# Attention scores stored through a second DMA queue, and a weight product computed in another order from an earlier step

## The chip, the cores and the metric

The kernel runs on one core of one Trainium2 chip. The metric is the device time of one execution in microseconds (us); lower is better. Three runs of the kernel before took 1441.49, 1444.0 and 1446.57 us, median 1444.0.

## The reference

Attention with two mixings across heads, then a gated expert network whose last two weights have nothing between them (batch 8, 12 heads, 448 rows, head width 64; model width 768, inner width 1024):

```python
scores = scale * np.matmul(q, k.transpose(0, 1, 3, 2))
scores = np.einsum('bhij,hg->bgij', scores, w_pre)
scores = scores - np.max(scores, axis=-1, keepdims=True)
attn = np.exp(scores)
attn = attn / (np.sum(attn, axis=-1, keepdims=True) + 1e-09)
attn = np.einsum('bhij,hg->bgij', attn, w_post)
x = np.matmul(attn, v)                 # (8, 12, 448, 64) -> (3584, 768)
a = x @ w1
b = x @ w2
h = a * b @ w3
out = h @ w_out
```

The weights w1, w2, w3 and w_out are float64 on the host and reach the chip as pairs of 32-bit words. The kernel makes a float32 of each value, and of that a high and a low part in float32r.

## The kernel before

**The loop.** The attention goes in steps, 45 for each batch of ten score rows over all 12 heads, 360 in all; `run` writes the order of every engine's instructions out by hand. Batch 0's first score tiles are made ahead of the loop. A step issues, in this order: at even steps the fetch of two later row tiles from DRAM (`fetch`, line 202, tiles r); what was put off in the list `later` (score stores among it); loads of the rest of batch 0's kq, of v and of later kq; the first half of one weight conversion; the minimum over a row tile (even steps) or the scaling (odd); the second half of the conversion; some background matmuls; the exponentials (line 235, even steps); more background matmuls; the products with v (lines 301) at a few odd steps; at odd steps the post matmuls of the last pair (line 260) and the pre-mix of the next (line 220); and last the score units of this step.

**Score units.** A unit (`qk`) is two heads by 128 score rows: eight matmuls (line 174) into two PSUM banks, two copies on ScalarE into a tile st (lines 179 and 180), and a store to DRAM (`raw_d`, lines 185 and 188). A batch has 21 units, six sets of three and three smaller ones that store in two pieces. The tiles st come from rings of two. The store isn't issued where the copies are: `qk` returns it as a function, the loop puts it into `later`, and the next step issues it on SyncE's queue (SP) behind the fetch. All transfers of the kernel go out on SP. Batch 0's units go one to a step at steps 0 to 14; batch 1's begin at step 11, one every 4/3 steps; each batch's kq loads come six steps ahead of their first unit.

**The fold.** w3 and w_out are multiplied into one weight while the attention of batch 0 runs. `fold_jobs` lists 40 loads and conversions: the first eighth of w3's columns (three jobs), w_out in two halves of columns of eight jobs each, the other seven eighths of three jobs each. `converting` makes one a step (squaring and a cast on ScalarE, four passes on VectorE, the low part on GpSimd, line 130), save at steps with v products. `folding` then makes, for each eighth and each half of w_out's columns, 24 matmuls (line 360): eight blocks of the inner width, three products of parts each. 16 groups make 384 matmuls. The result goes through a tile fz to DRAM.

**The planner.** Three things decide how many fold matmuls a step gets. `shares(FOLD, SWITCH - 1, ...)` (line 847) deals all but 24 of them over steps 18 to 48 so that the steps come out level against the score units, v products and post and mix matmuls they also have. `there(p)` (line 865) caps what is done by the conversions made up to the step before; p counts the conversions. The first 24 may go ahead of the dealing. At step 50 (`SWITCH`) the fold must be done; the expert network's matmuls follow as background.

**Ahead of the loop**, rows 0 to 47 of batch 0's first score tiles are stored first, and the other 80 rows of all heads by one transfer (line 805, called at 881) behind the first two fetches.

Of the kernel before, what the change touches and what calls it, by code (L numbers as in the profile page):

```python
# [6 lines left out]
F32 = mybir.dt.float32  # L7
F32R = mybir.dt.float32r
I32 = mybir.dt.int32
AF = mybir.ActivationFunctionType  # L10
ALU = mybir.AluOpType
# [9 lines left out]
NB = -(-S // IB)  # L21
QT, NJ = 128, 4
GB = 15
NG = NB // GB
KF, K1 = FF // 128, DM // 128
IH = IB // 2
HK = H * IH
PP = 64
JB = S // PP
SETS = NB * B // 2  # L30
FIRST = 48
CW = 384
DH = DM // 2
LATE = 2 * NB + GB + 2
PAIRS = ((0, 0), (0, 1), (1, 0))
# [15 lines left out]
class Kernel:  # L51
# [114 lines left out]
    def qk(self, b, p, c, banks):  # L166


        nc = self.nc
        ps = [self.bank(i, f"psq{b}_{p}_{c}_{s}")[:, :S] for s, i in enumerate(banks)]  # L170
        for z, (t, q, k) in enumerate(self.parts(b, p, c)):
            for s in range(2):
                rows = slice(s * D, (s + 1) * D)
                nc.tensor.matmul(ps[s][z * PP:(z + 1) * PP], t[rows, q:q + PP], t[rows, k:k + S], start=True, stop=True)  # L174
        if b == c == 0:
            st = self.sz[:, 2 * p:2 * p + 2]
        else:
            st = (self.qp if b == 0 and p % 2 else self.kp).tile([128, 2, S], F32, tag="st", name=f"st{b}_{p}_{c}", bufs=2)
        nc.scalar.copy(st[:, 0], ps[0])  # L179
        (nc.vector.tensor_copy if b == c == 0 else nc.scalar.copy)(st[:, 1], ps[1])  # L180
        raw = self.raw_d[b]
        if c == 3:
            def store():
                for z in range(2):
                    nc.sync.dma_start(raw[3 * QT:, 2 * (p + z) - 2:2 * (p + z)], st[z * PP:(z + 1) * PP])
            return store
        n = QT if b or c else FIRST
        return lambda: nc.sync.dma_start(raw[c * QT:c * QT + n, 2 * p:2 * p + 2], st[:n])

# [137 lines left out]
    def fold_jobs(self):  # L329
        self.fo = self.fp.tile([128, KF, 2, DM], F32R, tag="o", name="fo", bufs=1)  # L330
        w3 = self.w_src[2].rearrange("(k p) f -> p k f", p=128)
        columns = [[(w3[:, k, f * 256:(f + 1) * 256], lambda x, f=f, k=k: self.fold_part(x, f, k))
                    for k in (slice(0, 3), slice(3, 6), slice(6, 8))] for f in range(KF)]
        yield from columns[0]
        for q in range(2):
            for k in range(KF):
                src = self.w_src[3][k * 128:(k + 1) * 128, 2 * q * DH:2 * (q + 1) * DH]
                hi, lo = (self.fo[:, k:k + 1, t, q * DH:(q + 1) * DH] for t in range(2))
                yield src.rearrange("p (a n) -> p a n", a=1), lambda x, hi=hi, lo=lo: self.two_parts(x, hi, lo)
        for f in range(1, KF):  # L340
            yield from columns[f]

    def fold_part(self, x, f, k):
# [2 lines left out]
        self.two_parts(x, *(self.fw[f][:, k, t] for t in range(2)))  # L346

    def folding(self):
        nc = self.nc
        for f in range(KF):  # L350
            for half in range(2):
                w = self.fw[f]

                i = 6 + half
                p = self.bank(i, f"psf{half}_{f}")[:, :DH]
                atoms = [(k, t, x, y) for k in range(KF) for t, (x, y) in enumerate(PAIRS)]
                for k, t, x, y in atoms:
                    if (k, t) != (0, 0):
                        yield
                    nc.tensor.matmul(p, w[:, k, x], self.fo[:, k, y, half * DH:(half + 1) * DH],  # L360
                                     start=(k == 0 and t == 0), stop=(k == KF - 1 and t == 2))
                z = self.fp.tile([128, 3, 2, 128], F32R, tag="z", name=f"fz{half}_{f}")
                q = p.rearrange("p (d c) -> p d c", c=128)
                dst = self.w34_d[half * 3:(half + 1) * 3, :, f].rearrange("d p t c -> p d (t c)")

                def low(z=z, q=q, dst=dst):
                    nc.vector.tensor_tensor(z[:, :, 1], q, z[:, :, 0].bitcast(F32), op=ALU.subtract)
                    self.later.append(lambda: nc.sync.dma_start(dst, z.rearrange("p d t c -> p d (t c)").bitcast(F32)))

                self.ends.append((i, lambda z=z, q=q: nc.scalar.copy(z[:, :, 0], q)))  # L370
                self.soon.append((i, low))
                yield

# [365 lines left out]
    def run(self):  # L741
        nc, tc = self.nc, self.tc
# [33 lines left out]
        w = self.kp.tile([128, 2, S], F32, tag="st", name="wpre_s", bufs=2)[:, 0, :PP]  # L776
# [18 lines left out]
        held = []  # L795
# [6 lines left out]
        next(fold_pieces)  # L802
        for f in held:
            f()
        held = lambda: nc.sync.dma_start(self.raw_d[0][FIRST:QT], self.sz[FIRST:])

# [1 line left out]
        for n, u in enumerate([(0, p, c) for c in (1, 2) for p in range(HP)] + [(0, p, 3) for p in range(1, HP, 2)]):  # L810
            qks[n] = [u]
        for b in range(1, B):
            first, per = (11, 28 / 21) if b == 1 else ((b - 1) * NB - 6, NB / 21)
            units = [(b, p, c) for g in range(0, HP, 2) for p, c in [*itertools.product((g, g + 1), range(3)), (g + 1, 3)]]
            for i, (b, p, c) in enumerate(units):
                n = int(first + i * per) | (b > 1)
                qks.setdefault(n, []).append((b, p, c))
                if c == 0:
                    loads.setdefault(max(n - 6, 0), []).append((b, p))
        for b in range(B):  # L820
            for a in range(NG):
                for g in range(HP):
                    n = (b * NB + (a + 1) * GB + 3) | 1
                    avs.setdefault(n if g < 3 else n + 2, []).append((b, a, g))

        N = B * NB
        FOLD, SWITCH, E_AT = 18, NB + 5, NB + 8
        PAIR, P_AT = 4 * NB + 7, 4 * NB + 15
        P_1 = 7 * 3 * (2 * K1 // 2 * KF // 2 + KF // 2 * K1 // 2)
        E_1, E_2 = 2 * KF * K1 * 3, K1 * KF * 3  # L830
# [18 lines left out]
        for pair in range(ONE // 2, B // 2 - 1):  # L849
            first = P_AT if pair == ONE // 2 else 2 * NB * (pair + 1) + 13  # L850
# [3 lines left out]
        background, total, done = self.folding(), F_N, 0  # L854
# [9 lines left out]

        def there(p):

            f, r = divmod(p - 3 - 2 * KF, 3)
            return 2 * KF * 3 * (1 + f) + (0, 9, 18)[r] if f >= 0 else min(max(3 * (p - 3), 0), KF * 3)

        wanted, LF = 0, 4  # L870
        self.v_list = [(b, g) for b in range(B) for g in range(HP)]
# [6 lines left out]
            self.fetch(m)  # L878
        next(fold_pieces)
        next(fold_pieces)  # L880
        held()
        next(fold_pieces)
        next(fold_pieces)
        self.mix(0)
# [4 lines left out]
        for n in range(N + 6):  # L889
# [4 lines left out]
            if n == SWITCH:  # L894
# [10 lines left out]
                background, total, done = self.experts(phases), (E_1 + E_2) * ONE + P_1 * (B - ONE) // 2, 0  # L905
# [29 lines left out]
            p, pieces = self.n_made - 1 if fold_pieces else 2 * KF + 3 * KF, None  # L935
            if avs.get(n):
                pass
            elif fold_pieces:
                f = (self.n_made - 1 - 2 * KF) // 3
                if f < 2 or done >= 2 * KF * 3 * (f - 1):  # L940
                    pieces = fold_pieces
                    if next(pieces, self) is self:
                        fold_pieces = pieces = None
# [18 lines left out]
            if n < SWITCH:  # L962

                wanted += now
                now = max(min(there(p), KF * 3 + wanted) - done, 0)
# [13 lines left out]
                self.mix(m + 1)  # L979
            self.do_ends()  # L980
            for i, x in enumerate(qks.get(n, [])):
                self.later.append(self.qk(*x, (6, 7) if i else (0, 1)))
            if third:
                next(unit_pieces)

# [66 lines left out]
```

## Time and profile before

| what | value |
|---|---|
| median of three runs | 1444.0 us (1441.49 to 1446.57) |
| the profiled execution | 1437.83 us, span 1436.1 us |
| TensorE matmul busy | 1382.4 us (96%) |
| ScalarE, VectorE, GpSimd busy | 832.4, 741.1, 620.3 us |
| mean granted TensorE clock | 0.986 |
| transfers | 416.87 MB, mean 290 GB/s |

The numbers come from one execution, profiled on the chip. Where a row has a start and a duration, both are in us from the start of the span. PE is TensorE's matmul row, PEld its weight loads, DVE VectorE, ACT ScalarE, POOL GpSimd, SP SyncE; SPq is SP's queue, which mostly issues transfers. A busy share is an average over stages, and busy TensorE isn't TensorE at full clock: PEclk tells what clock the throttle granted. A view by stretches gives, for each stretch, busy time and instruction count of each engine, the clock, the busy share of the 16 transfer engines and GB/s. A row of waits reads "engine line <- releaser: us in total, times, longest".

### The profile page before, as it was taken

What the parts mean: (1) busy time and instruction counts of PE and PEld (TensorE: products, weight loads), DVE (VectorE), ACT (ScalarE), POOL (GpSimd) and SP (SyncE); (2) the same over time, 40 slices, a digit from 0 to 9 for tenths busy, and PEclk for the clock granted to TensorE, in tenths of its full rate; (3) what the DMA queues carried; (4) which work ended last, traced back from release to release, by engine and by line L of the source; (5) the groups of instructions that cost most, each with busy time, mean ns of one, the idle gap of its engine ahead of it and who ended that gap; (6) DMA issues with size and microseconds to landing.
All of it is one profiled execution on the core that took longest, in us unless ns stands there. A gap on an engine that the chain in (4) does not pass through costs nothing.

```text
span 1436.1 us, 45775 instructions
## 1 busy us (share of the span) xinstructions
PE 1382.4 (96%) x18684; PEld 1055.2 (73%) x18684; DVE 741.1 (52%) x1497; ACT 832.4 (58%) x1952; POOL 620.3 (43%) x754
## 2 busy tenths in 40 slices
PE   5889999999999999999999999999999999999998
PEld 2457786776677667776777777777777777899988
DVE  6867566767544544432444436334444446345563
ACT  4867666777766666665656556556555445422231
POOL 2433233434433544532345336334335446446693
PEclk7989999999999999999999999999999999999999
DMA  8998789999999999999989979799879757698775
GB/s 294 366 326 279 236 270 322 320 312 317 324 286 348 355 356 330 362 346 349 287 275 290 320 259 280 249 323 354 288 229 281 241 177 223 195 337 270 231 232 171
DMA packets 203761, 416.87 MB, mean 290 GB/s; under 512 B 20528, under 2 KB 120112, under 8 KB 203472
## 3 DMA queue, kind: packets, MB, share of 16 engines
q1 hardware_dynamic: 203552, 413.94, 87.6%
q8 instruction: 149, 2.44, 0.7%
q14 instruction: 60, 0.49, 0.1%
HBM read 279.77 MB, written 134.09 MB: 288 GB/s over the span
## 4 chain that ended last, share of the span: by engine, by line
PE 82%; DMA 8%; DVE 4%; ACT 2%; issue 1%; POOL 1%; SPq 0%; DVEq 0%; POOLq 0%; ACTq 0%
PE e L702 21%; PE psa L301 11%; PE pso L260 10%; PE psm L220 9%; PE psq L174 7%; PE eg L522 5%; PE psf L360 4%; PE eo L553 4%; PE e2o L702 4%; PE e1o L702 4%; PE e3o L702 4%; DMA wu<-w_d 3%; DMA r<-raw_d 2%; DMA raw_d<-st 2%; ACT e L235 1%
## 5 line engine op out<-in xcount | busy, mean ns | idle before, releaser
L247 POOL TENSOR_SCALAR w<-wpo,ri 128x60 f32<-128x60 f32 x360 | 180.7, 518 | 485.1 <-DVE ri L245 465.3
L227 DVE TENSOR_REDUCE mn<-psm 128x1 f32<-128x448 f32 x360 | 207.7, 618 | 321.6 <-PE psm L220 321.3
L274 ACT COPY mt<-pso 128x480 f32<-128x480 f32 x352 | 197.9, 621 | 185.8 <-PE pso L260 185.6
L702 PE MATMUL e<-eh,wu 128*128 128x448 f32 x1008 | 296.8, 371 | 6.4 <-DVE c L656 3.2
L235 ACT ACTIVATE e<-psm,mn 128x448 f32<-128x448 f32 x360 | 226.8, 643 | 7.9 <-DVE mn L227 7.9
L702 PEld LDWEIGHTS e<-eh,wu 128*128 128x128 f32 x1008 | 187.5, 188 | 52.2 <-issue 26.8
L260 PEld LDWEIGHTS pso<-w,e 60*64 60x64 f32 x10080 | 175.2, 135 | 51.0 <-issue 42.5
L220 PE MATMUL psm<-r,wsc 60*64 60x448 f32 (+1 forms) x1440 | 191.2, 550 | 19.1 <-DVE cx L124 8.3
L260 PE MATMUL pso<-w,e 60*64 60x60 f32 x10080 | 199.1, 224 | 0.4 <-ACT mt L274 0.3
L702 PE MATMUL e<-el,wu 128*128 128x448 f32 x504 | 186.9, 371 | 0.0
L301 PE MATMUL psa<-mt,v 128*64 128x150 f32 (+1 forms) x2304 | 156.9, 292 | 4.1 <-ACT st L179 4.1
L301 PEld LDWEIGHTS psa<-mt,v 128*64 128x64 f32 x2304 | 143.6, 137 | 20.1 <-ACT st L179 6.7
L174 PE MATMUL psq<-kq 64*64 64x448 f32 x1176 | 154.6, 542 | 2.4 <-ACT st L179 2.4
L656 DVE TENSOR_TENSOR c<-c,e 128x448 f32<-128x448 f32 x168 | 101.7, 618 | 87.7 <-PE e L702 82.9
L179 ACT COPY st<-psq 128x448 f32<-128x448 f32 x162 | 86.4, 533 | 73.7 <-ACT mt L274 34.1
L522 PE MATMUL eg<-xh,wu 128*128 128x448 f32 x384 | 119.2, 381 | 6.3 <-DMA wu<-w_d 6.3
L641 POOL TENSOR_TENSOR el<-x,eh 128x448 fp32r<-128x448 f32 x90 | 103.7, 1170 | 32.8 <-ACT eh L640 29.9
L702 PEld LDWEIGHTS e<-el,wu 128*128 128x128 f32 x504 | 94.6, 188 | 22.5 <-issue 14.1
L174 PEld LDWEIGHTS psq<-kq 64*64 64x64 f32 x1176 | 60.8, 135 | 56.4 <-issue 28.8
L522 PEld LDWEIGHTS eg<-xh,wu 128*128 128x128 f32 x384 | 71.9, 190 | 38.7 <-issue 24.0
L244 DVE TENSOR_SCALAR sa<-sm 128x2 f32<-128x2 f32 x180 | 34.9, 194 | 113.6 <-ACT e L235 113.1
L180 ACT COPY st<-psq 128x448 f32<-128x448 f32 x162 | 87.6, 541 | 0.0
(99 smaller groups left out, 2010.1 us busy)
## 6 DMA issues: line engine op xcount, KB each, us to landing
r<-raw_d SPq DMA_DIRECT2D x344, 210.0 KB, 5.1
raw_d<-st SPq DMA_DIRECT2D x138, 448.0 KB, 6.1
wu<-w_d SPq DMA_DIRECT2D x104, 384.0 KB, 6.7
wu<-s_d SPq DMA_DIRECT2D x96, 384.0 KB, 4.8
wu<-w_d SPq DMA_DIRECT2D x51, 512.0 KB, 5.5
kq<-kq SPq DMA_DIRECT2D x42, 448.0 KB, 7.0
wu<-s_d SPq DMA_DIRECT2D x36, 512.0 KB, 4.9
x<-x_d SPq DMA_DIRECT2D x72, 224.0 KB, 5.7
```

The source lines that it names most:

```text
L174: nc.tensor.matmul(ps[s][z * PP:(z + 1) * PP], t[rows, q:q + PP], t[rows, k:k + S], start=True, stop=True)
L220: nc.tensor.matmul(ps[s][c * PP:(c + 1) * PP, :S], self.wsc[k], r[k, c], start=True, stop=True)
L227: self.nc.vector.tensor_reduce(mn[:, s:s + 1], self.psm[m][s][:, :S], axis=AX.X, op=ALU.min)
L235: nc.scalar.activation(e, p[:, :S], AF.Exp, bias=mn[:, s:s + 1], scale=-1.0, accum_out=sm[:, s:s + 1])
L247: nc.gpsimd.tensor_scalar_mul(w2[:, s], self.wpo, ri[:, s:s + 1])
L260: nc.tensor.matmul(self.pso[c][z * PP:(z + 1) * PP, at:at + HK], e[k, j * PP:(j + 1) * PP], w2s[k, s], start=True, stop=True)
L274: self.nc.scalar.copy(dst.rearrange("p j g (s i) -> p j s g i", s=2), src)
L301: nc.tensor.matmul(self.psa[rows, g % 3, :W], v[:, j, rows], mt[:, j, 2 * g + s, :W], start=(j == 0), stop=(j == NJ - 1))
L522: nc.tensor.matmul(p, u[:, k % (K1 // 2), x], xs[y][:, k], start=(k == 0 and t == 0), stop=(k == K1 - 1 and t == 2))
L641: nc.gpsimd.tensor_tensor(lo, x, hi.bitcast(F32), op=ALU.subtract)
L656: nc.vector.tensor_tensor(a[out], a[to[0]], p, op=ALU.add)
L702: nc.tensor.matmul(p, w[:, k, x], ops[m, k][y], start=(k == 0 and t == 0), stop=(k == nk - 1 and t == 2))
```

## The change

Three things are edited.

1. *Stores.* For batch 0 (all but its first score tiles) and batch 1 the store is issued with `nc.scalar.dma_start`, on ScalarE's own queue, right after the unit's copies and in the same step. Batches 2 to 7 keep the list `later` and SP. The 80 rows ahead of the loop go out on ScalarE's queue as well, in two pieces, rows 48 to 63 and 64 to 127.
2. *The fold's order.* Weights come as: first eighth of w3, first half of w_out, second eighth, second half of w_out, the other eighths. The groups are first eighth by first half; second eighth by first half; then both eighths by second half, alternating block by block in two banks; then as before. `there` and the condition under which conversions go on follow that order.
3. *The dealing.* `FOLD` goes from 18 to 9, and batch 1's units start at step 15 instead of 11, one every 1.15 steps instead of every 4/3.

```diff
-        raw = self.raw_d[b]
+        raw, dma = self.raw_d[b], nc.sync.dma_start if b > 1 or b == c == 0 else nc.scalar.dma_start
...
-        held = lambda: nc.sync.dma_start(self.raw_d[0][FIRST:QT], self.sz[FIRST:])
+        held = [lambda k=k: nc.scalar.dma_start(self.raw_d[0][k], self.sz[k]) for k in (slice(FIRST, PP), slice(PP, QT))]
...
-        yield from columns[0]
         for q in range(2):
+            yield from columns[q]
             for k in range(KF):
...
-        for f in range(1, KF):
+        for f in range(2, KF):
             yield from columns[f]
...
+        for group in [((0, 0),), ((1, 0),), ((0, 1), (1, 1))] + [((f, half),) for f in range(2, KF) for half in range(2)]:
+            banks = {g: 6 + (g[0] if g[0] < 2 else g[1]) for g in group}
+            ps = {g: self.bank(banks[g], f"psf{g[1]}_{g[0]}")[:, :DH] for g in group}
+            for k in range(KF):
+                for f, half in group:
+                    for t, (x, y) in enumerate(PAIRS):
+                        self.nc.tensor.matmul(ps[f, half], self.fw[f][:, k, x], self.fo[:, k, y, half * DH:(half + 1) * DH],
+                                              start=(k == 0 and t == 0), stop=(k == KF - 1 and t == 2))
+                        if (k, t) == (KF - 1, 2):
+                            self.fold_out(f, half, banks[f, half], ps[f, half])
+                        yield
...
-            first, per = (11, 28 / 21) if b == 1 else ((b - 1) * NB - 6, NB / 21)
+            first, per = (15, 1.15) if b == 1 else ((b - 1) * NB - 6, NB / 21)
...
-        FOLD, SWITCH, E_AT = 18, NB + 5, NB + 8
+        FOLD, SWITCH, E_AT = 9, NB + 5, NB + 8
...
-            f, r = divmod(p - 3 - 2 * KF, 3)
-            return 2 * KF * 3 * (1 + f) + (0, 9, 18)[r] if f >= 0 else min(max(3 * (p - 3), 0), KF * 3)
+            f, r = divmod(p - 6 - 2 * KF, 3)
+            if f >= 0:
+                return 2 * KF * 3 * (2 + f) + (0, 9, 18)[r]
+            if p >= 6 + KF:
+                return 2 * KF * 3 + 6 * (p - 6 - KF)
+            return KF * 3 + (0, 9, 18)[p - 3 - KF] if p >= 3 + KF else 3 * max(p - 3, 0)
...
-                if f < 2 or done >= 2 * KF * 3 * (f - 1):
+                if f < 2 or done >= 2 * KF * 3 * max(f - 1, 2):
...
-                self.later.append(self.qk(*x, (6, 7) if i else (0, 1)))
+                store = self.qk(*x, (6, 7) if i else (0, 1))
+                if x[0] > 1:
+                    self.later.append(store)
+                else:
+                    store()
```

`fold_out` holds the copy, the low part and the store of a group's result as `folding` had them.

More of the change, by code (lines that the diff above doesn't have):

```diff
@@ L180, in qk, with store @@
         (nc.vector.tensor_copy if b == c == 0 else nc.scalar.copy)(st[:, 1], ps[1])
-        raw = self.raw_d[b]
-        if c == 3:
-            def store():
+        raw, dma = self.raw_d[b], nc.sync.dma_start if b > 1 or b == c == 0 else nc.scalar.dma_start
+        def store():
+            if c == 3:
                 for z in range(2):
[L185 to L188, printed above, removed]
+                    dma(raw[3 * QT:, 2 * (p + z) - 2:2 * (p + z)], st[z * PP:(z + 1) * PP])
+            else:
+                n = QT if b or c else FIRST
+                dma(raw[c * QT:c * QT + n, 2 * p:2 * p + 2], st[:n])
+        return store
     def width(self, n):
@@ L348, in folding @@
     def folding(self):
-        nc = self.nc
[L350 to L372, printed above, removed]
@@ new lines, in fold_out, with low @@
+    def fold_out(self, f, half, i, p):
+        nc = self.nc
+        z = self.fp.tile([128, 3, 2, 128], F32R, tag="z", name=f"fz{half}_{f}")
+        q = p.rearrange("p (d c) -> p d c", c=128)
+        dst = self.w34_d[half * 3:(half + 1) * 3, :, f].rearrange("d p t c -> p d (t c)")
+        def low():
+            nc.vector.tensor_tensor(z[:, :, 1], q, z[:, :, 0].bitcast(F32), op=ALU.subtract)
+            self.later.append(lambda: nc.sync.dma_start(dst, z.rearrange("p d t c -> p d (t c)").bitcast(F32)))
+        self.ends.append((i, lambda: nc.scalar.copy(z[:, :, 0], q)))
+        self.soon.append((i, low))
@@ L880, in run @@
         next(fold_pieces)
-        held()
+        for f in held:
+            f()
         next(fold_pieces)
@@ L981, in run @@
             for i, x in enumerate(qks.get(n, [])):
-                self.later.append(self.qk(*x, (6, 7) if i else (0, 1)))
+                store = self.qk(*x, (6, 7) if i else (0, 1))
+                if x[0] > 1:
+                    self.later.append(store)
+                else:
+                    store()
             if third:
```

## The prediction

> **What bounds the kernel now.** I read the busy times by stretch first. A step's time is read from its post matmuls (line 260), which run at odd steps: step 1 ends with mix 1 at 24.2 us, step 9 posts at 52.74, step 19 at 99.52, step 39 at 181.16, step 51 at 225.66.
>
> ```profile
> core 0: us, PE busy (x) PEld busy (x) DVE busy (x) ACT busy (x) POOL busy (x), PEclk, DMA share, GB/s
> ...
> 24.22:52.74 28.52, 25.25 (x288) 11.55 (x289) 24.42 (x48) 23.24 (x57) 12.34 (x16) 0.83 1.00 345
> 52.74:99.52 46.78, 36.18 (x485) 21.31 (x484) 33.53 (x66) 32.31 (x78) 16.48 (x21) 0.82 1.00 357
> 99.52:181.16 81.64, 80.37 (x1125) 62.02 (x1123) 52.68 (x108) 54.88 (x131) 23.49 (x36) 1.00 0.81 258
> 181.16:225.66 44.50, 43.84 (x652) 35.82 (x651) 26.48 (x57) 27.94 (x68) 11.16 (x17) 1.00 0.85 269
> ```
>
> Call the last three A, B and C. In B and C TensorE is busy 98% at a clock of 1.00. In A the transfers are (share 1.00), and TensorE runs at a granted clock of 0.82 with 10.6 us idle. The edit's work ends at step 50, and what follows (1210 us) is dealt by the same lines; I let a gain made by step 51 stand to the end. Same view, the fold's matmuls alone:
>
> ```profile
> 52.74:99.52 46.78, 3.66 (x20) 3.27 (x19) 0.82 1.00 357
> 99.52:181.16 81.64, 41.61 (x219) 37.52 (x219) 1.00 0.81 258
> ```
>
> So A holds 19 of the 384 fold matmuls, although it is where TensorE stands idle. Next the waits inside A, then the chain of waits there:
>
> ```profile
> ACT st L179 <- DMA raw_d<-st: 8.8, 4, 4.1
> PE psq L174 <- ACT st L179: 6.8, 6, 2.1
> ```
> ```profile
> 55.01 5.68 DMA r<-raw_d
> ...
> 71.09 7.26 DMA raw_d<-st
> ```
>
> The score copy waits for a buffer whose store hasn't landed, and TensorE for the copy. The transfers view of A gives sizes (448 KB is 0.459 MB, also that of a kq load, 128 x 896 x 4 bytes):
>
> ```profile
> DMA packets 8296, 16.69 MB, mean 357 GB/s; under 512 B 797, under 2 KB 4671, under 8 KB 8292
> ...
> raw_d<-st SPq DMA_DIRECT2D x11, 448.0 KB, 7.2
> ```
>
> How stores and loads get out, from the timeline of SP's queue and, below it, of ScalarE:
>
> ```profile
> 52.26 0.33 SPq L103 DMA_DIRECT2D cs<-wo  x1
> 54.62 0.81 SPq L202 DMA_DIRECT2D r<-raw_d  x2
> 55.47 0.39 SPq L188 DMA_DIRECT2D raw_d<-st  x1
> 55.91 0.43 SPq L286 DMA_DIRECT2D v<-v  x1
> 56.44 0.61 SPq L103 DMA_DIRECT2D cs<-wo  x1
> 57.43 0.33 SPq L188 DMA_DIRECT2D raw_d<-st  x1
> 58.10 0.33 SPq L286 DMA_DIRECT2D v<-v  x1
> 59.51 0.33 SPq L157 DMA_DIRECT2D kq<-kq  x1
> ...
> 69.36 1.38 SPq L202 DMA_DIRECT2D r<-raw_d  x2
> 71.09 1.30 SPq L188 DMA_DIRECT2D raw_d<-st  x2
> ...
> 90.76 1.58 SPq L202 DMA_DIRECT2D r<-raw_d  x2
> 96.71 0.35 SPq L188 DMA_DIRECT2D raw_d<-st  x1
> ```
> ```profile
> 64.90 0.54 ACT L180 COPY st<-psq 128x448 f32<-128x448 f32 x1
> ```
>
> The copy that ended at 65.44 had its store issued at 71.09 at the earliest, 5.6 us later, behind the fetch of 69.36. And SP's own waits in A hold this:
>
> ```profile
> SPq L157 <- DMA cs<-wo: 1.1, 1, 1.1
> ```
>
> The kq load of 59.51 shares no data with a weight load; it is the eighth issue after the cs load of 52.26. I read it as a limit of eight transfers in flight: the ninth waits for the landing of the first, whichever engine issues it. On SP such a wait costs no compute; on ScalarE it would.
>
> **The change, part by part.** Durations at full clock, from the chain of waits in B, where one thing follows the other on TensorE:
>
> ```profile
> 131.94 1.01 PE pso L260 x54
> 132.95 0.77 PE psm L220 x8
> 133.71 0.75 PE psq L174 x8
> 134.47 2.81 PE psf L360 x15
> 137.27 0.91 PE psq L174 x8
> ...
> 153.75 3.28 PE psa L301 x48
> ```
>
> A pair of steps costs 1.78 (post and mix), a score unit 0.83 (between 0.75 and 0.91), a fold matmul 0.187, a group of AV 3.28. Now the planner. Carrying its sums through for the code before gives 24 fold matmuls done by step 9, 43 by 19, 262 by 39, 384 by 48: 24, then the rows' 19 and 219, then 122. For the code after, the shares dealt from step 9 run ahead of the weights, so the arrival function decides: nothing gains on step 9 (24 done), and at step 19 conversion 21 allows 48 + 6 x (21 - 14) = 90. Then 284 by step 39 and 384 by 48. So A gets 66 instead of 19, B 194 instead of 219, C 100 instead of 122. Score units: batch 1 from step 15 instead of 11 makes 10 in A instead of 12, 17 in B instead of 15.
>
> *C.* 22 x 0.187 = 4.1 us less, on a TensorE that is busy throughout: gain 4.1. ScalarE is busy 27.9 of 44.5 and the transfers 0.85, so both bear 40.4.
>
> *B.* Before: 10 x 1.78 + 15 x 0.83 + 219 x 0.187 + 3 x 3.28 = 81.1, against 81.64 in the row. After: 17.8 + 14.1 + 36.3 + 9.8 = 78.0, so 78.5 with the same 0.5 between: gain 3.1 if TensorE stays the bound. Against it: the folds come in lumps (none at steps 20 and 22, 30 at step 25), each as late as its weights, and the transfers rise: 258 GB/s x 81.64 is 21.1 MB, plus two units (0.9), about three weight loads (1.2) and whatever A leaves behind (1.4): 24.6 MB in 78.5 us are 313 GB/s. Ends: +3.1 and -2.0 (one step of idle at a low clock); I take 2.0, nearer the upper, as 313 stays under the 357 that A shows.
>
> *A.* TensorE needs 8.9 + 8.3 + 66 x 0.187 + 3.28 = 32.8 at full clock, so it doesn't bound. With three folds a step TensorE was granted 0.83 over steps 1 to 9, so the clock may recover in part. The transfers bound: 16.69 MB, less two stores (0.92), plus one more fold result (0.39), makes 16.2, or 45.3 us at 357 GB/s. But A before began with eight transfers in flight and ended with fewer (SP's list shows eight issues within one landing time at the start, and none from 92.3 to 96.7); if it now ends as it began, some 1.4 MB (three to four transfers) pass into B, and 14.8 MB take 41.4. Between 41.4 and 45.3 I take 42.5, since stores that needn't pass SP's fetches keep the transfers fed: gain 4.3.
>
> The issues on ScalarE: ten units in A, three of them with two stores, 13 x 0.33 to 0.45 (SP's rows) are 4 to 6 us. ScalarE has 32.3 busy there, less 2 x 1.08 for the copies that moved: 30.1 + 5 = 35 of 42.5, so they hide behind the transfers. Were that cover gone, they would cost the 5 whole. The wait of each store for its own two copies (0.54) is on ScalarE as well, and behind it queue the next step's weight casts and exponentials.
>
> *Steps 1 to 9.* Eight issues, 0.33 to 0.45 each, are 3 us on a ScalarE that is busy 23.2 of 28.5; part shows: loss 1.0 (0 to 3). The kq load that step 5 made goes behind step 9: 0.459 MB at 345 GB/s, gain 1.3. The small one-time edit before the loop:
>
> ```profile
> SPq L202 <- DMA raw_d<-sz: 5.5, 3, 4.5
> ```
>
> SP held everything for up to 4.5 us until rows 48 to 127 had landed; now the fetch of rows 40 to 59 needs only rows 48 to 63, which go first. The bytes stay, and the transfers are at 1.00 right after: gain 1.0 (-1 to 4.5).
>
> The order of the fold's groups, its use of the two banks and the condition on conversions add no instruction; I count them as nothing, hidden by the lag of one step between a conversion and its matmuls.
>
> Sum: 1.0 + 1.3 - 1.0 + 4.3 + 2.0 + 4.1 = 11.7 us. The profiled execution took 1437.8 (span 1436.1 and 1.7 around it), so 1426.1 on its scale; the median of the runs is 1444.0, 6.2 higher, so **1432** there. Its own range is 1427 to 1437 (A at 41.4 or 45.3, B at its ends).
>
> **The rivals.** *The bytes alone decide.* The transfer engines are at a share of 1.00 over A, so stores that go out sooner only push loads back. Then A falls to 45.3 and no further, the one-time edit gives nothing, and the sum is 1.3 - 1.0 + 1.5 + 2.0 + 4.1 = 7.9, or 1436. Against it: SP issued nothing for 4.4 us at the end of A. Chance 0.17. The Trainium skill ("DMA: Bandwidth & Descriptors", section "Issuing engines are not separate DMA queues") states the same: transfers run on one set of 16 engines and interleave whoever issues them, and a second issuer saves only issue time. Before, all of them come from SP, so this trace can't show whether that holds.
>
> *The stores get through sooner than I think.* If a queue of their own is served beside SP's backlog of seven transfers, buffers come free early and A comes down to ScalarE's 35 to 36: gain 10.5 there, 18 to 20 in all, or 1425. Stores that take 7.2 us to land, behind everything else, speak for it; the 357 GB/s against. Chance 0.10.
>
> *ScalarE stands in the transfer limit: slower.* In A each store on ScalarE waits until the transfer eight before it has landed, with exponentials and casts queued behind. SP's stores came up to 5.6 us after their copies. ScalarE has 42.5 - 30.1 = 12.4 us to give for 13 stores: from 0.95 us a store on, issue included, it decides. At 2 us of wait and 0.4 of issue A would be 30.1 + 31 = 61, 14.5 longer, and steps 1 to 9, where there is less to give, 2 longer yet on balance; less B and C (6.1), and 1.3 from kq: +9, or 1453. Against: SP can now run ahead of a store, and in-flight slots free at the same pace as before. Chance 0.15.
>
> *It doesn't do what it says.* The folds of A hang on weights converted one step before; if each step now waits for GpSimd's low part as TensorE orders it ahead of the scores, about 1 us a step goes, A stays near 46.8, B gains nothing, issue costs show fully (3), and only C's 4.1 and kq's 1.3 are left: -2, or 1442. Chance 0.13. My forecast has 0.45.
>
> **How the numbers follow.** A measurement of this kernel can tell about 0.3%, 4.3 us, from no change: faster is under 1439.7, slower over 1448.3. Faster: 0.43 of the forecast, 0.10, and 0.12 of the bytes case: 0.65. Same: 0.02, 0.05, 0.10 of the last and 0.03 of the ScalarE case: 0.20. Slower: the rest, 0.15. The range runs from 1422 to 1447; beyond it lie most of the ScalarE case and little of the second.
>
> **What would show it.** Right: between the post matmuls of steps 9 and 19, 66 folds and some 42 to 43 us; 78 to 81 from there to step 39; 40 to 41 to step 51; ScalarE's waits for st down from 8.8. Wrong: transfers of weights or of r becoming what ScalarE's queue waits for at lines of the store, with A over 47; or a granted clock still near 0.8 in A; or a step 51 as late as 225.

## The result and the profile after

The changed kernel takes 1463.25 us, the median of four runs (1456.77 to 1464.69), against 1444.77 for four runs of the kernel before: a ratio of 1.0123, 95% interval 1.0092 to 1.0153. It is slower, where 1432 was predicted. Its profiled execution took 1464.69 us.

The page of the kernel after, busy times, clock and the transfer queues (q1 is SP's, q10 is ScalarE's; packets, MB, share of the 16 engines):

```profile
span 1462.9 us, 45722 instructions
...
PE 1392.1 (95%) x18684; PEld 1056.3 (72%) x18684; DVE 740.3 (51%) x1497; ACT 833.8 (57%) x1952; POOL 617.2 (42%) x754
...
q1 hardware_dynamic: 198176, 395.70, 83.4%
q10 hardware_dynamic: 5392, 18.24, 3.5%
```

ScalarE's busy time has hardly risen (832.4 before), because time spent on issuing transfers is not counted as busy. The page alone hides the cost. The stretches show it. From here on a step's time is the start of its pre-mix, which follows the post matmuls at once: step 1 at 30.36, step 9 at 60.95, step 19 at 112.64, step 39 at 203.77, step 51 at 244.57.

The view by stretches of the kernel after (steps 1 to 9, then A, B and C):

```profile
30.36:60.95 30.59, 25.00 (x342) 12.31 (x346) 28.07 (x55) 24.14 (x58) 13.52 (x18) 0.94 1.01 345
60.95:112.64 51.69, 42.59 (x528) 26.59 (x522) 31.57 (x62) 30.86 (x73) 15.22 (x21) 0.87 0.83 278
112.64:203.77 91.13, 82.36 (x1126) 59.68 (x1122) 56.53 (x117) 58.65 (x138) 24.66 (x36) 0.96 0.80 248
203.77:244.57 40.80, 40.14 (x642) 32.25 (x636) 20.70 (x47) 26.36 (x64) 8.53 (x16) 1.00 0.82 266
```

With the same marks before (24.22, 53.60, 100.38, 182.03, 226.52) the four stretches took 29.38, 46.78, 81.65 and 44.49 us. So 6.1 us are lost ahead of step 1, 1.2 in steps 1 to 9, 4.9 in A and 9.5 in B; C gives 3.7 back. At step 51 the kernel is 18.05 us late, which agrees with 18.5 between the medians. (Between the two profiled executions another 8.8 appear after that, in work the edit doesn't touch; the one of before lies 7 under its median.)

In A the transfers are now at 0.83 instead of 1.00, and TensorE is busy for 42.6 of 51.7 us: neither is the bound. The fold's matmuls alone, same view:

```profile
60.95:112.64 51.69, 18.42 (x66) 12.76 (x66) 1.10 (x2) 0.93 (x2) 0.87 0.83 278
112.64:203.77 91.13, 40.53 (x194) 34.16 (x194) 4.79 (x9) 4.16 (x9) 0.96 0.80 248
203.77:244.57 40.80, 18.76 (x100) 17.17 (x100) 2.78 (x5) 2.43 (x5) 1.00 0.82 266
```

The dealing came out as predicted, 66, 194 and 100. In A a fold matmul takes 18.42 / 66 = 0.279 us, in C 0.188. What TensorE waits for between 25 and 245 us, in the waits of the kernel after:

```profile
PE psm L223 <- DMA r<-raw_d: 15.9, 1, 15.9
PE psf L358 <- ACT fw L129: 7.8, 3, 3.7
PE psf L358 <- POOL fo L130: 7.5, 12, 1.1
```

Before, TensorE waited most for the score copies (6.8 us), and its folds 1.9 us for low parts (line 130). Now the folds wait 15.3 us for a weight's cast on ScalarE or its low part on GpSimd. The chain of waits shows why; a part of it in A:

```profile
59.46 8.09 DMA cs<-wo
...
67.63 0.33 ACTq L189
...
68.00 0.52 ACT fw L129
...
68.58 1.02 POOL fw L130
...
69.65 2.61 PE psf L358 x7
72.25 1.74 PE pso L263 x56
```

The store's issue on ScalarE (ACTq) waits for a weight load that was issued on SP and shares no data with it. The trace's records say why: each transfer signals one of eight semaphores, which SP's and ScalarE's transfers use in turn. The store's, number 101, is that of the cs load of 59.46, the eighth transfer before it, and the issue waits until that has landed. Behind the store stands the cast of a weight, behind the cast GpSimd's low part, behind that the fold's matmuls, and behind these, in TensorE's order, the post matmuls and the rest of the step.

But such waits are few. The timeline of ScalarE, an ordinary store and one in two pieces:

```profile
60.09 0.53 ACT L180 COPY st<-psq 128x448 f32<-128x448 f32 x1
60.66 0.33 ACTq L189 DMA_DIRECT2D raw_d<-st  x1
61.02 0.51 ACT L129 CAST fw<-cx 128x384 fp32r<-128x384 f32 x1 [0.40 <-ACT st L180]
...
67.63 0.33 ACTq L189 DMA_DIRECT2D raw_d<-st  x1
68.00 0.51 ACT L129 CAST fw<-cx 128x384 fp32r<-128x384 f32 x1 [3.77 <-DMA cs<-wo]
...
86.19 0.54 ACT L180 COPY st<-psq 128x448 f32<-128x448 f32 x1
86.76 1.15 ACTq L186 DMA_DIRECT2D raw_d<-st  x2
87.95 0.51 ACT L129 CAST fo<-cx 128x384 fp32r<-128x384 f32 x1 [1.23 <-DVE cx L123]
```

Before, the operation behind a second copy began 0.43 us after it, while the copy still ran (the copy is the prediction's row at 64.90):

```profile
65.33 0.53 ACT L129 CAST fo<-cx 128x384 fp32r<-128x384 f32 x1
```

Now it is 0.93 (60.09 to 61.02), because the issue starts only when the copy has ended and takes 0.33: 0.5 us more for each store. A store in two pieces costs 87.95 - 86.19 - 0.43 = 1.33. In A, of ten units, one cost 3.9 us for the landing at 67.6, five cost 0.50 to 0.53, three in pieces 1.30 to 1.33, and one was followed by a wait for TensorE anyway: 3.9 + 2.6 + 3.9 = 10.4 us in which ScalarE did nothing else. In B the same reading gives 10.2 in 14 of the 17 units (the other three were followed by waits for TensorE); there no store began more than 0.04 us after its copy, so none waited for a landing.

### The profile page after: what moved, and what is told of

Same layout as the page of the kernel before. It is cut to its first block, busy times and chain, and to the rows that moved or that the text cites. A ratio compares the mean times of both kernels' runs of the same rounds, so it can differ in the third digit from the quotient of the medians.

```text
span 1462.9 us, 45722 instructions
## 1 busy us (share of the span) xinstructions
PE 1392.1 (95%) x18684; PEld 1056.3 (72%) x18684; DVE 740.3 (51%) x1497; ACT 833.8 (57%) x1952; POOL 617.2 (42%) x754
## 4 chain that ended last, share of the span: by engine, by line
PE 81%; DMA 9%; DVE 4%; ACT 4%; issue 1%; POOL 1%; ACTq 1%; SPq 0%; DVEq 0%; POOLq 0%
PE e L705 20%; PE psa L304 11%; PE pso L263 10%; PE psm L223 9%; PE psq L174 7%; PE eg L525 5%; PE psf L358 4%; PE e2o L705 4%; PE e1o L705 4%; PE e3o L705 4%; PE eo L556 4%; DMA r<-raw_d 2%; DMA wu<-w_d 2%; ACT e L238 1%; DMA cs<-wo 1%
## 5 line engine op out<-in xcount | busy, mean ns | idle before, releaser
L304 PEld LDWEIGHTS psa<-mt,v 128*64 128x64 f32 x2304 | 144.2, 137 | 18.5 <-issue 6.4
L179 ACT COPY st<-psq 128x448 f32<-128x448 f32 x162 | 86.3, 533 | 71.4 <-PE psq L174 33.6
L358 PEld LDWEIGHTS psf<-fo,fw 128*128 128x128 f32 x384 | 68.1, 196 | 52.4 <-POOL fo L130 10.7
L358 PE MATMUL psf<-fo,fw 128*128 128x384 f32 x384 | 86.2, 365 | 19.4 <-ACT fw L129 7.8
```

The lines of the kernel that those rows point to most:

```text
L304: nc.tensor.matmul(self.psa[rows, g % 3, :W], v[:, j, rows], mt[:, j, 2 * g + s, :W], start=(j == 0), stop=(j == NJ - 1))
L358: self.nc.tensor.matmul(ps[f, half], self.fw[f][:, k, x], self.fo[:, k, y, half * DH:(half + 1) * DH], start=(k == 0 and t == 0), stop=(k ...
```

## The experiments

Two theories come from this. *Landings*: ScalarE stands at a store until an older transfer has landed (the eighth before it, as the prediction read it), and without such waits the change would be worth its price. *Issues*: every store takes half a microsecond or more of an engine that lies on the loop's own chain, and that decides, landings or not. Rivals beside them are the edit ahead of the loop, the fold's new order with its one-step-old weights, and batch 1's later units. (In the expectations a theory 1 is that of landings; theories 2 and 3 put the loss down to folds that wait for their weights, and a theory 4 is that of issues.)

Offsets against the profiled execution of before, in us, at the start of a step's pre-mix:

| kernel | step 1 | step 9 | step 19 | step 29 | step 51 | median | ratio (95%) |
|---|---|---|---|---|---|---|---|
| after | +6.1 | +7.4 | +12.3 | +21.8 | +18.1 | 1463.25 | 1.0123 (1.0092 to 1.0153) |
| e1_held_back | +0.3 | +7.4 | +14.8 | +25.6 | +21.8 | 1463.61 | 1.0116 (1.0083 to 1.0150) |
| e2_stores_sp | +6.4 | +4.7 | +1.1 | +6.5 | +1.1 | 1446.52 | 1.0017 (1.0002 to 1.0032) |
| e3_both_sp | +0.1 | +2.2 | -0.6 | +6.4 | +0.9 | 1444.71 | 1.0015 (0.9999 to 1.0031) |
| e4_stores_only | -0.5 | +9.3 | +6.5 | +7.3 | +7.2 | 1451.78 | 1.0050 (1.0030 to 1.0071) |
| e6_sp_at_once | +0.4 | +0.9 | -1.2 | +4.3 | +2.9 | 1447.71 | 1.0035 (1.0019 to 1.0050) |
| e7_pool | +0.7 | +3.4 | +0.7 | +9.9 | +5.8 | 1448.83 | 1.0040 (1.0025 to 1.0055) |
| e9_lag | +5.7 | +7.8 | +7.1 | +17.8 | +13.6 | 1460.48 | 1.0120 (1.0099 to 1.0140) |
| e10_late_units | +0.1 | +1.0 | -3.8 | +2.0 | -1.4 | 1444.36 | 1.0004 (0.9988 to 1.0019) |
| e11_units_only | -0.1 | +0.9 | 0.0 | +1.2 | +3.6 | 1447.72 | 1.0025 (1.0008 to 1.0042) |
| e12_act_next | +0.4 | +7.3 | +9.1 | +18.7 | +14.6 | 1457.76 | 1.0084 (1.0060 to 1.0109) |
| e13_even | -0.3 | +0.7 | -2.8 | +0.7 | -2.4 | 1442.31 | 0.9994 (0.9982 to 1.0006) |
| e14_b1_act | +0.6 | +1.6 | +4.9 | +16.0 | +12.3 | 1454.73 | 1.0066 (1.0046 to 1.0086) |

The kernel before, measured beside them on three chips, had medians of 1443.67 (e1 to e4), 1443.06 (e6, e7, e9, e10) and 1443.12 (e11 to e14).

### The edit ahead of the loop undone (e1)

```diff
-        held = [lambda k=k: nc.scalar.dma_start(self.raw_d[0][k], self.sz[k]) for k in (slice(FIRST, PP), slice(PP, QT))]
+        held = [lambda: nc.sync.dma_start(self.raw_d[0][FIRST:QT], self.sz[FIRST:])]
```

> The changed kernel, but the 80 rows ahead of the loop go out on SP in one transfer at their old place. The comparison of the two traces has the first pre-mix 7.7 us later and the second 6.1 later; both theories (ScalarE standing in the limit of eight transfers; folds waiting for weights) put this part down to those rows having passed the first fetches. So mix 1 back to 24 to 25 us and 5 to 7 us less than the changed kernel: about 1457.

1463.61 us, no gain in the time, where some 6 were expected. The edit does cost something where it acts. Before, SP issued the first four fetches and then the 80 rows (80 x 12 x 448 x 4 bytes, 1.72 MB):

```profile
14.95 1.74 SPq L202 DMA_DIRECT2D r<-raw_d  x4
...
17.18 0.42 SPq L805 DMA_DIRECT2D raw_d<-sz  x1
```

In the kernel after, ScalarE has issued both pieces before SP comes to the fetches,

```profile
13.02 0.35 ACTq L808 DMA_DIRECT2D raw_d<-sz  x1
...
14.22 0.50 ACTq L808 DMA_DIRECT2D raw_d<-sz  x1
```

and the four fetches, now behind them, take 6.72 us to issue instead of 1.74:

```profile
14.88 6.72 SPq L205 DMA_DIRECT2D r<-raw_d  x4
```

TensorE's first pre-mix waits 15.9 us for a fetch (its row stands above), begins at 25.87 instead of 18.16, and step 1 begins 6.1 us late. With the rows back on SP it begins 0.3 late, and yet at step 9 both kernels are 7.4 late: in e1 the stores take in steps 1 to 9 what the late start took here. A part of that is waits for landings: at the stores of these steps they are 4.1 and 0.7 us in e1, 1.6 and 0.6 in the kernel after (a third, in A, is 3.7 and 3.4). The edit is worth nothing in the sum, and is not the cause.

### The unit stores back on SP (e2), and both (e3)

```diff
-        raw, dma = self.raw_d[b], nc.sync.dma_start if b > 1 or b == c == 0 else nc.scalar.dma_start
+        raw, dma = self.raw_d[b], nc.sync.dma_start
...
-                if x[0] > 1:
-                    self.later.append(store)
-                else:
-                    store()
+                self.later.append(store)
```

> The changed kernel, but the stores of the score units go back to SP and to the next step; the two pieces ahead of the loop stay on ScalarE. Theory 1 (each store on ScalarE waits for the landing of the transfer eight before it and holds up the engine): the loss between steps 1 and 30 goes, steps 9 to 39 take less than 125 us, 1440 to 1446. Theory 2 (the folds dealt from step 9 wait for weights converted a step before, whoever stores): no more than 4 us come back, about 1459.

> Only the fold's new order and the dealing from step 9 with batch 1's units from step 15; every transfer on SP as before. Theory 1: faster than before by 6 to 11 us, 1434 to 1439. Theory 2: 1450 or more.

1446.52 and 1444.71 us: with the unit stores on SP the kernel falls by 17 us, and the intervals stand far apart. All of the loss beyond a microsecond or three is theirs. What is left, the fold's order and dealing with the later units, is no gain either: e3 came out between what the two theories had for it. The view by stretches of e3 (A, steps 19 to 23, 23 to 29, B, C):

```profile
55.76:99.82 44.06, 38.36 (x525) 23.77 (x520) 32.51 (x63) 30.54 (x73) 16.86 (x22) 0.95 1.01 352
99.82:117.48 17.66, 14.46 (x229) 9.68 (x225) 11.67 (x24) 11.40 (x27) 5.57 (x7) 0.92 0.72 226
117.48:146.83 29.35, 28.31 (x345) 21.23 (x340) 19.87 (x40) 19.20 (x46) 9.04 (x12) 0.99 0.83 267
99.82:186.84 87.02, 81.38 (x1128) 59.02 (x1122) 58.17 (x117) 57.93 (x138) 26.91 (x36) 0.98 0.82 260
186.84:227.46 40.62, 39.96 (x642) 31.84 (x636) 20.97 (x47) 26.39 (x64) 8.53 (x16) 1.00 0.85 268
```

Against it the kernel before, steps 19 to 23 and 23 to 29:

```profile
100.38:117.81 17.43, 16.79 (x255) 13.09 (x249) 11.30 (x23) 11.25 (x27) 4.96 (x7) 1.00 0.72 217
117.81:140.42 22.61, 22.61 (x316) 16.76 (x310) 17.83 (x37) 17.14 (x41) 7.82 (x12) 1.00 0.96 318
```

A gains 2.7 and C 3.9 us, but B loses 5.4. Steps 19 to 23 hold 15 fold matmuls instead of 41, as no more weights are there, and take as long: TensorE stands idle for 3.2 us instead of 0.6. Steps 23 to 29 then hold 94 instead of 70, and take 6.7 us longer.

### The stores alone, on the kernel before (e4)

```diff
-        raw = self.raw_d[b]
+        raw, dma = self.raw_d[b], nc.sync.dma_start if b > 1 or b == c == 0 else nc.scalar.dma_start
...
-                self.later.append(self.qk(*x, (6, 7) if i else (0, 1)))
+                store = self.qk(*x, (6, 7) if i else (0, 1))
+                if x[0] > 1:
+                    self.later.append(store)
+                else:
+                    store()
```

> The kernel before, with the score stores of batches 0 and 1 on ScalarE's queue at once; fold, dealing and the rows ahead of the loop as before. Theory 1: 8 to 15 us slower than before, 1452 to 1459, with ScalarE's queue waiting for landings at the stores' lines. Theory 2: within 0.3% of before.

1451.78 us, some 8 slower than before. All of it is lost by step 9. Up to there two of ScalarE's stores wait for landings, 4.1 and 1.7 us, so here the landings are most of the loss (a third wait, of 1.2, follows at 68.4). A then takes 43.98 instead of 46.78, and B and C what they took. So where A has few folds, the stores cost nothing that shows there, and the loss is of steps 1 to 9. With the other edits they cost 19 (e1 against e3): the two parts make each other worse. That the folds of one-step-old weights, which stand right behind ScalarE, are how they do so fits the chain above; e9 puts it to a test.

### The engine that issues: SP at once (e6), GpSimd (e7)

Both have the edit ahead of the loop undone, and issue the unit stores in the step of their copies as the change does.

```diff
-        raw, dma = self.raw_d[b], nc.sync.dma_start if b > 1 or b == c == 0 else nc.scalar.dma_start
+        raw, dma = self.raw_d[b], nc.sync.dma_start                                                     # e6
+        raw, dma = self.raw_d[b], nc.sync.dma_start if b > 1 or b == c == 0 else nc.gpsimd.dma_start    # e7
```

> The changed kernel with the stores of the score units issued in their own step as there, but on SP, and the rows ahead of the loop as before. Theory 1 (what costs is that ScalarE stands at the store until the transfer eight before has landed): as the kernel with all on SP, 1441 to 1448. Rival (the earlier place in the order of transfers costs, whoever issues): 1455 or more.

> The changed kernel with the stores of the score units on GpSimd's queue in place of ScalarE's, and the rows ahead of the loop as before. GpSimd's transfers have semaphores of their own, so no store waits for the landing of SP's transfers, but they still share the 16 engines from a second queue. Theory 1: 1441 to 1450, with some of GpSimd's time for the issues. Rival (a second queue takes the bandwidth from the loads): 1455 or more.

e6 takes 1447.71 us: the same place in the program, on SP, is 16 us under e1. So neither the earlier issue nor the transfers it brings forward cost much; the engine does. e7 takes 1448.83, with a second queue that also has stores beside SP's loads. GpSimd's timeline in it,

```profile
61.30 0.61 POOL L189 DMA_DIRECT2D raw_d<-st  x1 [0.96 <-ACT fw L129]
61.93 1.01 POOL L130 TENSOR_TENSOR fw<-cx,fw 128x384 fp32r<-128x384 f32 x1
```

has an issue of 0.61 us, longer than ScalarE's, ahead of the same low parts. But GpSimd had been idle before it, and is busy for only 15.2 of the 51.7 us of A in the kernel after. So a second queue in itself is not what costs 16 us.

### Older weights for the folds (e9)

```diff
-                now = max(min(there(p), KF * 3 + wanted) - done, 0)
+                now = max(min(there(p - (2 if p < 22 else 0)), KF * 3 + wanted) - done, 0)
```

> The changed kernel, but up to conversion 21 a step's fold matmuls use only weights converted three steps before, not one. Theory 3 (a held-up ScalarE casts weights late, and the folds that wait for them hold up the post, mix and score matmuls behind them on TensorE): the stretch from step 9 to 19 falls by 4 us or more from 51.7, about 1457. Theory 1 alone (the held-up ScalarE itself sets the pace): within 2 us of the changed kernel, 1461 to 1465.

1460.48 us. With folds that use weights three steps old the stretch A falls from 51.69 to

```profile
61.44:107.43 45.99, 40.10 (x506) 23.66 (x510) 32.60 (x66) 32.31 (x77) 15.68 (x22) 0.89 0.92 313
```

with 60 of its fold matmuls in it instead of 66 (at 0.28 us each, 1.7 of the 5.7 us). The other 4.0 speak for the folds' waits as a part of the loss in A, which is 7.6 against e3. They are weak evidence, as the profiled execution is the fastest of four here (1457.93) and the slowest of four for the kernel after (1464.69). The total doesn't follow: the profile is 4.5 us ahead of the kernel after at step 51, but the ratio to the kernel before is 1.0120, as good as unchanged. TensorE's waits (25 to 241 us) show what takes the folds' place: the folds now wait 4.5 us for casts and low parts instead of 15.3, but the score matmuls 7.0 for score copies (2.4 in the kernel after) and the pre-mixes 5.1 for the exponentials (0.4). All of these are ScalarE's work.

### Landings or issues: batch 1's stores alone on ScalarE (e14), and issues a step later (e12)

```diff
-        raw, dma = self.raw_d[b], nc.sync.dma_start if b > 1 or b == c == 0 else nc.scalar.dma_start
+        raw, dma = self.raw_d[b], nc.scalar.dma_start if b == 1 else nc.sync.dma_start
...
-                if x[0] > 1:
+                if x[0] != 1:
```

> All on SP but the stores of batch 1's units (steps 15 to 38), which go out on ScalarE at once; fold and dealing as in the changed kernel. In the changed kernel's trace no store after step 15 waits for a landing (0.03 us each). Theory 1 (only the landing counts): within 2 us of the kernel with all on SP, 1443 to 1447. Theory 4 (the issue itself, about 0.5 us of ScalarE for each of 24 transfers): 4 to 9 us above it, 1449 to 1454.

> The changed kernel with the rows ahead of the loop on SP, and the stores of the score units still on ScalarE's queue, but issued in the next step (behind the fetch in the order of transfers, with the copies long done). Theory 1 (the wait for a landing eight transfers back): the wait comes at a later place, but eight transfers back is later too, so about the same, 1458 to 1464. Theory 4 (each issue costs ScalarE about 0.5 us in its row, 0.33 of issue and the rest until its own copies have drained, and the row is on the loop's chain): the drain goes, the issue stays, 1452 to 1458.

e14, which like e3 has the edit ahead of the loop undone, takes 1454.73 us. No store on ScalarE waits for a landing there, and it is still 0.5% slower than e3, with the intervals apart. So landings are not needed for the loss. But they are not out of it. At step 51 e14 is 11.4 us behind e3, and e1, which has batch 0's stores on ScalarE as well, 20.8: a good half of the loss comes with batch 1's stores and without a landing, the other 9.4 us with batch 0's, among which e1 has waits for landings of 8.5. The ratios (1.0015, 1.0066, 1.0116) divide it the same way. How much of the second half the landings are isn't shown, as no run has batch 0's issues without them.

e14's rows for A and B,

```profile
55.16:105.32 50.16, 41.22 (x526) 26.42 (x522) 32.58 (x66) 31.06 (x74) 15.97 (x22) 0.86 0.89 316
105.32:198.18 92.86, 84.19 (x1128) 61.43 (x1122) 56.43 (x117) 58.54 (x138) 24.71 (x36) 0.94 0.77 243
```

lose 6.1 and 5.8 us on e3's, and in its chain of waits the store of 0.33 us stands in the same place:

```profile
95.18 0.33 ACTq L189
...
95.55 0.52 ACT fo L129
...
96.14 1.01 POOL fo L130
...
97.19 1.97 PE psf L358 x5
99.16 5.37 PE psa L304 x48
```

A holds four of these stores, some 2 us of ScalarE by the reading above, and is 6.1 us longer: the issue's own time isn't the whole price. The last row shows a second part of it: 48 matmuls that took 3.28 us at full clock before took 5.37, as for the most part the clock granted was 0.50:

```profile
97.00:103.00 6.00, 5.81 (x37) 5.15 (x39) 0.89 (x3) 1.59 (x6) 0.97 (x3) 0.50 0.39 150
```

Ahead of it, TensorE stood idle for 1.42 us until a score copy and for 0.63 until a low part. The Trainium skill ("TensorE: Matmul & The Clock Gate", section "HAM oscillation — how this bites in real kernels") describes bursts of about 2 us with waits of more than 3.4 us between them, after which the gate throttles TensorE again. Here the clock fell behind shorter waits. Over A it was 0.86 and 0.87, with the stores on SP 0.95.

e12 is the kernel of e1 with each store on ScalarE put off to the start of the next step (`self.later.append(store)` for all units). It was to take away the wait for the unit's own copies, and doesn't: the copies are ScalarE's last work in a step and the store its first in the next, so they stay neighbours in ScalarE's timeline,

```profile
60.31 0.56 ACT L180 COPY st<-psq 128x448 f32<-128x448 f32 x1
60.90 0.33 ACTq L189 DMA_DIRECT2D raw_d<-st  x1
61.27 0.51 ACT L129 CAST fw<-cx 128x384 fp32r<-128x384 f32 x1 [0.40 <-ACT st L180]
```

with the same 0.5 us. It took 1457.76 us, and its interval overlaps e1's. The run doesn't tell the issue from the drain ahead of it.

### Later units (e10, e11), and folds dealt evenly (e13)

```diff
-            first, per = (15, 1.15) if b == 1 else ((b - 1) * NB - 6, NB / 21)
+            first, per = (18, 1) if b == 1 else ((b - 1) * NB - 6, NB / 21)                  # e10 and e13, on e3
...
-            first, per = (11, 28 / 21) if b == 1 else ((b - 1) * NB - 6, NB / 21)
+            first, per = (15, 1.15) if b == 1 else ((b - 1) * NB - 6, NB / 21)               # e11, on the kernel before
...
-                now = max(min(there(p), KF * 3 + wanted) - done, 0)
+                now = min(max(min(there(p), KF * 3 + wanted) - done, 0), 16)                 # e13
```

> The kernel with only the fold's order and dealing changed and all transfers on SP, with batch 1's units from step 18, one a step, in place of step 15 and every 1.15. It takes three stores of 0.46 MB out of the stretch from step 9 to 19 and gives TensorE score matmuls at steps 19 to 24, where few folds have their weights. If the transfers bound that stretch at 355 GB/s it falls by 3 to 4 us from 44.1 and the whole to about 1440, 0.3% under before; if not, 1444 as with step 15.

> The kernel before with batch 1's units from step 15 and one every 1.15 steps; fold, dealing and queues as before. If the transfers bound steps 9 to 19, two stores fewer there take 2 to 3 us from its 46.8, which the two more in the next stretch cost back at 0.83 each: the whole within 0.3% of before, 1441 to 1445.

> The kernel with the fold's order and dealing, all on SP, batch 1's units from step 18, and at most 16 fold matmuls a step (steps 25 and 28 had 30). If the 30-matmul steps cost because the next group finds its bank not yet emptied and the other engines wait behind them, steps 23 to 29 fall by 1 to 3 us from 29.4, and the whole to 1439 to 1442; if only TensorE's total counts, 1444 as before.

e10: 1444.36 us; A falls to 42.02 with three units fewer, and B takes them back (87.86). e11: 1447.72, 4.6 over the kernel before on that chip, where no difference was expected; at step 51 its profile is 3.6 late, and the 0.0 at step 19 puts that behind A, 3.2 of it into B. Batch 1's later start is a small loss by itself (interval from 1.0008). e13: 1442.31, the lowest of all but not faster than before by what the runs can tell. Its rows for steps 19 to 23, 23 to 29 and B,

```profile
97.55:114.06 16.51, 14.65 (x237) 9.10 (x232) 11.54 (x24) 12.14 (x29) 4.66 (x7) 1.00 0.64 201
114.06:141.10 27.04, 27.04 (x341) 20.24 (x337) 19.82 (x40) 19.11 (x46) 10.02 (x13) 1.00 1.01 330
97.55:183.49 85.94, 82.77 (x1150) 58.91 (x1146) 57.92 (x117) 60.26 (x144) 26.70 (x36) 1.00 0.86 277
```

have B 1.9 us under e10's: with at most 16 folds in a step steps 23 to 29 fall from 29.38 us to 27.04, as expected, but the folds that steps 19 to 23 couldn't take remain.

## Why the prediction was wrong

It had a gain of 11.7 us at step 51, and the profile shows a loss of 18.05, a difference of 29.75.

| term | predicted gain | measured gain | missed by |
|---|---|---|---|
| ahead of step 1 | 1.0 | -6.1 | 7.1 |
| steps 1 to 9 | 1.3 - 1.0 | -1.2 | 1.5 |
| A | 4.3 | -4.9 | 9.2 |
| B | 2.0 | -9.5 | 11.5 |
| C | 4.1 | 3.7 | 0.4 |

**The step that failed** is the cover given to the issues: "ScalarE has 32.3 busy there, less 2 x 1.08 for the copies that moved: 30.1 + 5 = 35 of 42.5, so they hide behind the transfers." A busy sum under the stretch's length was taken for slack. But ScalarE's copies, casts and exponentials are links of the loop's chain, and an issue ahead of a cast delays a fold and all that TensorE has behind it. e14, whose stores wait for no landing, loses 10 us on e3 all the same. The price was low as well: 4 to 6 us in A were 10.4. Of these 3.9 are one wait for a landing, which the forecast left to a rival; the other 6.5 were spent at eight units, as the issue also breaks the overlap of one ScalarE operation with the next, and a store in two pieces takes 1.3. Once these hold up A, the transfers no longer bound it (0.83). Of A's miss of 9.2, 7.6 go with the stores (51.69 against e3's 44.06); the rest lies within the ends of 41.4 to 45.3.

**The rival on the other side** had the place right (ScalarE, with casts queued behind) and the point from which it decides too high: "from 0.95 us a store on". The mean in A was 10.4 / 13 = 0.8, and the kernel was slower all the same: ScalarE's 30.9 us of work and these 10.4 fill 41 of A's 51.7, so a full ScalarE is not what decided. Its mechanism is real but rare: not 2 us of waiting for a landing at every store, but three such waits in 36 units, 5.6 us in all (1.6, 0.6, 3.4), all before step 11. Its 1453 was too low since it kept B's gain. The limit of eight transfers across both queues, which the prediction read from one row of SP, is what the eight shared semaphores make.

**B** was wrong even without the stores: e3's 87.02 against 79.6. "Against it: the folds come in lumps" was the right doubt with too small a price, 2.0 at the far end: the idle of steps 19 to 23 isn't filled, and the folds are paid in full after it. The order of the fold's groups, put at nothing, has a part in it: in B the folds of e3 wait 2.6 us for casts and low parts, which those of before don't wait for there. The rest (4.1, e3 to after) is the stores' again, 10.2 us on ScalarE.

**The edit ahead of the loop** was said to save a wait of SP, at worst at a cost of 1. That the 80 rows, on a queue of their own, would pass the first four fetches was not seen; they did, and the first pre-mix began 7.7 us late. In the sum the edit comes out at nothing (e1).

**The range** doesn't follow from the ends named for it: with A at 41.4 and B at +3.1 the sum gives 1430, with A at 45.3 and B at -2.0 it gives 1439, not 1427 and 1437. The measured time lies far outside either.

**Right** were C's 4.1 (3.7, and 3.9 in e3), the numbers of folds, the 14.8 MB of A (14.37 in the transfers view), and that the bytes stay: 345 GB/s in steps 1 to 9 before and after. The Trainium skill ("DMA: Bandwidth & Descriptors", section "Issuing engines are not separate DMA queues") has the transfers run on one set of engines whoever issues them, which agrees; it calls the saved issue time usually small, and here that time, moved to ScalarE, cost more than it saved.

**Open:** how the loss splits between waits and the lower clock that follows them; how much of batch 0's half is its waits for landings; the issue against the drain of the unit's own copies; and whether what e3 has left over the kernel before (1.0, interval from 0.9999) is a loss at all.

## What to carry to other kernels

A compute engine whose busy share leaves room can still have none for issuing transfers: ask what stands behind the issue in its order, and whether the loop's chain runs through that. Price an issue by the distance from the last operation before it to the first after it, not by its own duration, and count stores in pieces separately. A transfer that moves to another queue also passes those that it stood behind: ask what waits for them.

## What the runs showed of the hardware that was not expected

- An issue of 0.33 us on ScalarE cost 0.5, as it began only when the copy before it had ended, where compute operations there follow each other every 0.43 us with durations of 0.53. A store in two pieces cost 1.3 us in A, and in B its two issues alone took 2.03 (at 125.3), 1.48 (at 165.0) and 2.79 (at 202.9).
- A store on ScalarE's queue waited for a weight load from SP's (67.63, 3.77 us of idle). In this program the two queues share eight semaphores for their transfers; the stores that e7 issues from GpSimd signal eight others.
- The same stores issued from GpSimd, at 0.6 us each, left the kernel 15 us faster than from ScalarE (1448.83 and 1463.61).
